# Moving 34 reversing weight copies out of the head of a tuned backward kernel, with later tables, four side jobs per call and a second-group scaling

## The chip, the cores and the metric

One core of one Trainium2 chip. Times are device microseconds (us) of the whole program. Engines: PE is TensorE, DVE VectorE, ACT ScalarE, POOL GpSimd, SP SyncE; SP issues most of the DMAs and does nothing else here.

## The reference, cut to what matters

```python
def _fwd_reference(A_x, A_w_r, A_w_i, B_x, B_w_gate, B_w_up, B_w_down, gate_w):
    x = A_x                                   # [1, 2048, 576] bf16
    g = _sigmoid((x * gate_w).sum(-1, keepdims=True))
    a = irfft2(rfft2(x) * (A_w_r + 1j * A_w_i))        # A_w: [2048, 289]
    b = (_gelu(x @ B_w_gate) * (x @ B_w_up)) @ B_w_down # [576, 4608]
    return g * a + (1 - g) * b
# reference(): this output, and the gradients of all inputs but B_x for a given grad_out (dO)
```

The kernel computes the two-dimensional transforms as matrix products with tables of angles, and the gated network (FFN) with its gradients.

## The kernel before

**The head** (0 to 87 us) loads x and dO, then the first weight block of the FFN, transforms x along one axis and then the other ("angles" Y, then "V" tiles), and stores the V tiles to DRAM. All the tiles of the transform share a pool of 19 buffers. At the end of its code stands `wrev`: 34 DRAM-to-DRAM copies that put the second half of the columns of A_w into reversed row order. POOL gets to them early and issues them from 8 to 70 us.

```python
    def reversed_rows(eng, src, dst):
        s_, d_ = (a.rearrange("(m i) (h l) -> h i m l", i=T, h=2) for a in (src, dst))
        return [lambda i=i: eng.dma_start(d_[:, i], s_[:, T - i, ::-1]) for i in range(1, T)] + \
            [...]                              # two more for i = 0
    ...
    for t in range(T):                         # head
        x1[t]()                                # angles
        ...
        if t % 3 == 0 and t + 3 < T:
            build_R(nc, tb, unit, t + 3)       # a block of tables
        if t > 0:
            x2[t - 1]()                        # V products
    build_B(nc, tb, unit, res)
    run_late(tb)
    tail_table()
    for k, v in enumerate((A_w_r, A_w_i)):
        for move in reversed_rows(nc.gpsimd, v[:, HF:DF], wrev[k][:]):
            move()
```

One such copy has the shape 2 x 128 x 72: 256 rows of 144 bytes.

**The groups** (87 to about 1030 us): 18 groups of 256 FFN columns with four iterations each. I number these 72 iterations from 0, so the second group starts with iteration 4 and the third with iteration 8. An iteration computes `z` (from `wdT`, the transposed down weights) and `xy` on PE, the activation and its derivative on ACT and DVE, weight-gradient products of the group before, and some units of the transform. In its first three iterations a group also loads the next group's weights on SP: transposes in the second (L241, L242), and in the third the copies that put the result in place, which must wait for the transposes (L245, L248). `side` holds DVE work of the transform's middle part, in small jobs; `moves` holds copies like `wrev` for the reversed halves of two outputs.

```python
    def load_w(g, part):
        if part == 0: ...                                                # wgu: six loads
        elif part == 1:
            LD.dma_start_transpose(wts[g][1][:, 4:5, :], B_w_down[fsl, DCH[4][0]:D])   # L241
            LD.dma_start_transpose(wtmp[0][:], B_w_down[fsl, 0:512])                   # L242
        else:
            LD.dma_start(wdT[LO, 4, :], wdT[HI, 4, :])                                 # L245
            ... LD.dma_start(wdT[r, 2 * par:2 * par + 2, :], wtmp[0][...])             # L248, four
    ...
            def side_work():                   # called after each half's elementwise work
                for _ in range(3):
                    if side:
                        side.pop(0)()
    ...
            if m < 3 and g + 1 < NG:
                load_w(g + 1, m)
            if (g, m) in ((0, 3), (1, 0)):
                scale_dB(T // 2)
            for _ in range(3):
                if moves:
                    moves.pop(0)()
```

**The last part** (from about 1030 us) is the last group's rest and PE products of the second phase; nothing of the change touches it.

## Time and profile before

| | before |
|---|---|
| time, median of three runs | 1491.16 us (1490.65 to 1492.24) |
| PE busy | 95% of the profiled 1494.7 us |
| start of the first z product (iteration 0) | 87.10 us |
| start of the second group (iteration 4) | 128.84 us |
| start of the third group (iteration 8) | 186.94 us |

The starts are those of the first z product (L341 on PE) of each iteration, read off the trace. Below I call "lead" how much earlier an iteration starts than in the profiled run of the kernel before. The prediction shows the profile itself.

### The profile page before, as it was taken

To read this page: it belongs to the slowest core of one execution; us is meant where nothing else is said; L and a number is where in the kernel's file an instruction comes from. 1 tells how busy PE (TensorE), PEld (TensorE's weight loads), DVE (VectorE), ACT (ScalarE), POOL (GpSimd) and SP (SyncE) were. 2 spreads that over 40 slices of the span, in tenths; PEclk is the share of its full clock that TensorE was granted. 3 is DMA by queue.
4 is the path that set the end of the run, shared out by engine and by line. 5 is a ranking of instruction groups with operands and counts; after the bars stand their busy time and mean duration, and the time that the engine had idled before them with its cause. 6 is when DMAs were issued, how large, how long until landed. Compare 5 with 4: busy or idle time off the path is not lost.

```text
span 1494.7 us, 30032 instructions
## 1 busy us (share of the span) xinstructions
PE 1414.5 (95%) x11500; PEld 1050.8 (70%) x11586; DVE 887.8 (59%) x2356; ACT 697.2 (47%) x1380; POOL 172.1 (12%) x258
## 2 busy tenths in 40 slices
PE   4388999999999999998999999999999999999997
PEld 3255767767776776776677777777877777777775
DVE  6269777988898889867677777775000461212200
ACT  3267766666667767666667667664000000000000
POOL 6500011111111111111010010010000110000000
PEclk8699999999999999999999999999999999999998
DMA  9925454455565555446556546665999998878773
GB/s 167 75 76 132 118 147 128 122 136 129 137 155 128 132 141 135 114 103 144 139 133 160 143 127 154 161 143 138 274 199 194 209 213 159 167 158 170 153 150 67
DMA packets 550712, 217.87 MB, mean 146 GB/s; under 512 B 375368, under 2 KB 540424, under 8 KB 550568
## 3 DMA queue, kind: packets, MB, share of 16 engines
q1 hardware_dynamic: 537800, 194.03, 59.4%
q0 software_dynamic: 10960, 20.91, 6.0%
q8 instruction: 90, 1.47, 0.5%
q10 hardware_dynamic: 1808, 1.02, 0.2%
q14 instruction: 54, 0.44, 0.1%
HBM read 43.28 MB, written 96.22 MB: 93 GB/s over the span
## 4 chain that ended last, share of the span: by engine, by line
PE 77%; DVE 2%; issue 1%; DMA 0%; SPq 0%; ACT 0%; DVEq 0%
PE acc L1043 28%; PE wps L464 14%; PE xy L353 12%; PE wps L447 8%; PE z L341 7%; PE wps L477 2%; PE xy L348 2%; PE z L344 1%; PE pf L745 1%; PE pf L772 1%; PE pf L774 1%; DMA pin<-scr 0%; PE pf L695 0%; PE pf L696 0%; PE pf L698 0%
## 5 line engine op out<-in xcount | busy, mean ns | idle before, releaser
L1043 PEld LDWEIGHTS <-pin 128*128 128x128 bf16 x3456 | 338.0, 98 | 86.5 <-DMA pin<-scr 1.4
L353 PE MATMUL xy<-wgu,xT 128*128 128x512 bf16 x1066 | 257.9, 380 | 10.1 <-issue 8.3
L464 PEld LDWEIGHTS <-xn 128*128 128x128 bf16 x2304 | 225.1, 98 | 31.3 <-issue 0.2
L353 PEld LDWEIGHTS <-xT 128*128 128x128 bf16 x1152 | 106.9, 98 | 139.0 <-issue 31.8
L366 ACT ACTIVATE da<-z,omg 128x256 bf16<-128x256 f32 x288 | 113.3, 474 | 126.6 <-PE z L344 123.2
L1060 ACT COPY bo<-acc 128x288 f32<-128x288 f32 x32 | 12.8, 399 | 309.3 <-PE acc L1043 284.7
L447 PE MATMUL wps<-dB,A 128*128 128x288 bf16 x1152 | 152.7, 286 | 0.0
L341 PE MATMUL z<-wdT,dOT 128*128 128x256 bf16 x1152 | 141.1, 277 | 7.0 <-DMA wdT<-wtmp 4.4
L1043 PE MATMUL acc<-wd_all,pin 128*128 128x288 bf16 x1152 | 142.8, 286 | 1.1 <-DMA pin<-scr 1.1
L1043 PE MATMUL acc<-wgT,pin 128*128 128x288 bf16 x1152 | 143.6, 286 | 0.0
L1043 PE MATMUL acc<-wuT,pin 128*128 128x288 bf16 x1152 | 143.6, 286 | 0.0
L447 PEld LDWEIGHTS <-A 128*128 128x128 bf16 x1152 | 112.6, 98 | 34.9
L464 PE MATMUL wps<-dHg,xn 128*128 128x256 bf16 x1152 | 133.1, 273 | 0.0
L464 PE MATMUL wps<-dHu,xn 128*128 128x256 bf16 x1152 | 132.0, 273 | 0.0
L341 PEld LDWEIGHTS <-dOT 128*128 128x128 bf16 x1152 | 112.5, 99 | 26.2 <-issue 6.5
L1120 DVE SCALAR_TENSOR_TENSOR f32t<-gwf,dlog,b16t 128x576 f32<-128x576 f32 x16 | 13.1, 817 | 179.2 <-DMA b16t<-dxa_scr 179.2
L372 ACT ACTIVATE q<-xy 128x512 bf16<-128x512 f32 x144 | 86.1, 598 | 66.0 <-PE xy L353 62.3
L396 ACT ACTIVATE om<-s 128x512 bf16<-128x512 bf16 x144 | 92.0, 639 | 23.7 <-DVE s L380 23.6
L470 POOL DMA_DIRECT2D out_dram<-dw x67 | 48.9, 730 | 440.7 <-ACT dw L425 290.6
L397 ACT ACTIVATE s<-s 128x512 bf16<-128x512 bf16 x144 | 90.7, 630 | 4.6
L378 ACT CAST hu<-xy 128x512 bf16<-128x512 f32 x144 | 87.0, 604 | 0.0
L379 DVE TENSOR_SCALAR s<-q 128x512 bf16<-128x512 bf16 x144 | 41.9, 291 | 73.2 <-ACT q L372 72.5
(213 smaller groups left out, 1846.8 us busy)
## 6 DMA issues: line engine op xcount, KB each, us to landing
scr<-A SPq DMA_DIRECT2D x144, 128.0 KB
scr<-dHg SPq DMA_DIRECT2D x144, 128.0 KB
scr<-dHu SPq DMA_DIRECT2D x144, 128.0 KB
out_dram<-dw POOLq DMA_DIRECT2D x67, 128.0 KB, 2.9
wd_all<-in_B_w_down_dram SPq DMA_DIRECT2D x3, 1728.0 KB
out_dram<-dwd POOLq DMA_DIRECT2D x34, 144.0 KB, 3.2
wgu<-in_B_w_gate_dram SPq DMA_DIRECT2D x18, 256.0 KB
wgu<-in_B_w_up_dram SPq DMA_DIRECT2D x18, 256.0 KB
```

The source lines that it names most:

```text
L341: nc.tensor.matmul(zo(t), lhsT=dOT[:, ci, t, :], rhs=wdT[:, ci, :], start=(t % 4 < 2 and ci == 0), stop=False)
L353: nc.tensor.matmul(xy[k][:, t % 2, :], lhsT=xT[:, ci, t, :], rhs=wgu[:, ci, :], start=False, stop=(ci == 3))
L366: nc.scalar.activation(da[:, tt, :], z[:, tt, k, :], ACT.Copy, scale=omg32[:, t:t + 1])
L372: nc.scalar.activation(q[:], xy[:, :, 0:FG], ACT.Square)
L378: nc.scalar.copy(hu[:], xy[:, :, FG:2 * FG])
L379: V.tensor_scalar(s[:], q[:], A_GELU, 1.0, op0=ALU.mult, op1=ALU.add)
L396: nc.scalar.activation(om[:], s[:], ACT.Sigmoid, scale=-2.0 * C_GELU)
L397: nc.scalar.activation(s[:], s[:], ACT.Sigmoid, scale=2.0 * C_GELU)
L447: nc.tensor.matmul(wps[:, :288], lhsT=tl(0, t)[:, fch * P:(fch + 1) * P], rhs=dB[:, t, h * 288:(h + 1) * 288], start=(t == 0), stop=(t == ...
L464: nc.tensor.matmul(wps[:, cc, :], lhsT=xn[:, t, (c0 + cc) * P:(c0 + cc + 1) * P], rhs=tl(k, t), start=(t == 0), stop=(t == T - 1))
L470: wst[0].dma_start(ov[:, c0:c0 + TPB, fsl], dw[:])
L1043: nc.tensor.matmul(acc[:, :288], lhsT=src[:, r, :], rhs=w_of(r)[:, h * 288:(h + 1) * 288], start=(first and r == 0), stop=(last and r == F ...
```

## The change

It takes `wrev` out of the head and puts it on SP, five copies per iteration until all are out, in the seventh iteration; builds tables and V products one step later; moves the tail table into an empty slot of the transform; puts every second early V copy on ACT; scales dO in the second group, with the products that use it after it; spreads the output copies; and does four side jobs per call.

```diff
         if g == 0:
-            return [[w[0], tl_], [w[1], d[0]], [d[1], d[2], d[3]], [w[2], w[3]], []]
+            return [[w[0], tl_], [w[1], w[2]], d, [w[3]], []]
...
-                if src is xT or t < 8:
+                if src is xT or (t < 8 and t % 2):
                     V.tensor_copy(Vt[:], vps[:, :, :2 * HF])
...
-                    if p == T // 2 - 1:
-                        for k, v in enumerate((out_2, out_3)):
-                            moves.extend(reversed_rows(LD, orev[k][:], v[:, HF:DF]))
+                        moves.extend(reversed_rows(orev[k][:], (out_2, out_3)[k][:, HF:DF], [(T - i) % T for i in (i0, i0 + 1)]))
...
-        if t % 3 == 0 and t + 3 < T:
-            build_R(nc, tb, unit, t + 3)
+        if t % 3 == 1 and t + 2 < T:
+            build_R(nc, tb, unit, t + 2)
...
-        if t > 0:
-            x2[t - 1]()
+        if t > 1:
+            x2[t - 2]()
+    x2[T - 2]()
...
-    tail_table()
-    for k, v in enumerate((A_w_r, A_w_i)):
-        for move in reversed_rows(nc.gpsimd, v[:, HF:DF], wrev[k][:]):
-            move()
+    for i in range(T):
+        for k, v in enumerate((A_w_r, A_w_i)):
+            moves.extend(reversed_rows(v[:, HF:DF], wrev[k][:], [i]))
...
-                for _ in range(3):
+                for _ in range(4):
                     if side:
                         side.pop(0)()
...
-            if (g, m) in ((0, 3), (1, 0)):
+            if (g, m) in ((1, 0), (1, 1)):
                 scale_dB(T // 2)
-            for _ in range(3):
+            for _ in range(5 if pr < 8 else 2):
                 if moves:
                     moves.pop(0)()
```

`pr` is the number of the iteration.

More of the change, by code (lines that the diff above doesn't have):

```diff
@@ L548, in tail_table @@
         nc.gpsimd.memset(tb.At2[:], 0.0)
-        pool, tag = headps()
-        tp_ = pool.tile([P, 2, 1024], BF16, tag=tag, name="tp")
+        tp_ = pz.tile([P, 2, 1024], BF16, tag="z", name="tp")
         for c in range(2):
@@ L582, in tiles_of, with reversed_rows @@
         return t[:].rearrange("(m i) l -> m i l", i=T)
-    def reversed_rows(eng, src, dst):
+    def reversed_rows(src, dst, tiles):
         s_, d_ = (a.rearrange("(m i) (h l) -> h i m l", i=T, h=2) for a in (src, dst))
-        return [lambda i=i: eng.dma_start(d_[:, i], s_[:, T - i, ::-1]) for i in range(1, T)] + \
-            [lambda: eng.dma_start(d_[:, 0, 1:P], s_[:, 0, P - 1:0:-1]), lambda: eng.dma_start(dst[0:1], src[0:1])]
+        out = []
+        for i in tiles:
+            if i:
+                out.append(lambda i=i: LD.dma_start(d_[:, i], s_[:, T - i, ::-1]))
+            else:
+                out.append(lambda: LD.dma_start(d_[:, 0, 1:P], s_[:, 0, P - 1:0:-1]))
+                out.append(lambda: LD.dma_start(dst[0:1], src[0:1]))
+        return out
     a_dv = a_scr[:].rearrange("(m i) d -> m i d", i=T)
@@ L829 @@
     mid = mid_units()
-    fft = fg + [gap] * 5 + mid[:-2] + pa + mid[-2:] + [gap] * 2 + ia[:-4] + pb + ia[-4:] + ib
+    fft = fg + [tail_table] + [gap] * 4 + mid[:-2] + pa + mid[-2:] + [gap] * 2 + ia[:-4] + pb + ia[-4:] + ib
     fft_pos = [0]
@@ L954 @@
                 LD.dma_start(gwb[:], gate_w.partition_broadcast(P))
-            if (g, m) in ((0, 3), (1, 0)):
+            if (g, m) in ((1, 0), (1, 1)):
                 scale_dB(T // 2)
-            for _ in range(3):
+            for _ in range(5 if pr < 8 else 2):
                 if moves:
                     moves.pop(0)()
+            assert pr != 8 or not moves
             if done[0] == n_slots or (pr >= wgT_from and pr % 2 == 0 and len(wgT_all) < 20):
```

## The prediction

> **What bounds the kernel now.** I read the page first: engine shares, then the 40 slices. TensorE ("PE") is busy 95% of 1494.7 us, and from the third slice on its row stands at 9. So a microsecond can be won only where PE is idle, and that is nearly all at the start.
>
> ```profile
> PE   4388999999999999998999999999999999999997
> PEclk8699999999999999999999999999999999999998
> DMA  9925454455565555446556546665999998878773
> ```
>
> A slice is 37 us: PE is 40% and 30% busy in the first two, while DMA is at 90% in both. I then asked for busy time by stage: the load, the hole, the rest of the head, the first group of the FFN, the second.
>
> ```profile
> 0.00:20.00 20.00, 10.24 (x78) 7.30 (x79) 13.98 (x39) 9.48 (x18) 16.45 (x33) 0.83 0.89 257
> 20.00:58.00 38.00, 8.23 (x78) 6.20 (x77) 9.05 (x20) 5.86 (x10) 19.65 (x19) 0.66 1.14 64
> 58.00:87.00 29.00, 23.62 (x286) 18.23 (x286) 16.96 (x43) 16.49 (x27) 7.01 (x8) 0.85 0.63 74
> 87.00:129.00 42.00, 37.30 (x240) 22.17 (x244) 32.35 (x90) 32.56 (x63) 0.00 (x0) 0.96 0.39 108
> 129.00:187.00 58.00, 55.74 (x445) 39.86 (x448) 46.48 (x133) 39.99 (x78) 4.46 (x7) 1.00 0.44 121
> ```
>
> Columns: stretch, length, busy us of PE, weight loads, DVE, ACT, POOL, then clock, DMA share, GB/s. From 20 to 58 us PE works 8.23 of 38 us, and DMA is fully busy while it moves only 64 GB/s. The waits of that stretch say why PE stands, and the DMA queue's order of issue says why the store it waits for is late.
>
> ```profile
> PE fx L530 <- ACT Y L519: 30.6, 2, 29.2
> ACT Rt L152 <- DMA scr_x<-Vt: 28.1, 1, 28.1
> ...
> 19.97 3.62 SPq L241 DMA_TRANSPOSE wdT<-in_B_w_down_dram  x1
> 23.64 4.16 SPq L242 DMA_TRANSPOSE wtmp<-in_B_w_down_dram  x1
> 34.24 0.50 SPq L245 DMA_DIRECT2D wdT<-wdT  x1
> 39.25 6.83 SPq L248 DMA_DIRECT2D wdT<-wtmp  x4
> 46.18 34.00 SPq L541 DMA_DIRECT2D scr_x<-Vt  x14
> ...
> q1 hardware_dynamic: 3333, 1.53, 67.8%
> q0 software_dynamic: 1842, 0.86, 45.3%
> ```
>
> The FFT's tiles share 19 "unit" buffers; about 29 us in, they are all taken by V tiles waiting to be stored. The stores stand behind the first weight block on the in-order SP queue: the issue of L245 waits for a transpose to land, L248 for the next, and the first scr_x store goes out at 46.18 and frees a buffer at 55.5. Meanwhile the 34 reversing copies of A_w (wrev, issued by POOL from 8 to 70 us) hold 45.3% of the DMA engines' time. The same block for the second group, without wrev, runs: transposes issued at 113.17 and 114.40, L245 at 123.47, L248 in 2.64 us. So the hole is DMA contention passed on through buffers.
>
> **What the Trainium skill says.** (1) "DMA: Bandwidth & Descriptors", section "Issuing engines are not separate DMA queues": DMAs of all issuers end on the same 16 engines and interleave. The trace agrees: both queues together are booked at 113% from 20 to 58 us. (2) The same page, "Why a DMA increments its semaphore by 16 and not by 1": an SP-issued DMA is split over the largest k up to 16 that divides the slowest non-unit dimension of both patterns. A reversing copy is 2x128x72, so k = 2: its 256 rows of 144 B go to two engines. The kernel already issues such copies from SP, for its outputs; the trace agrees by rate: in 641 to 642 us, when little else runs, the hardware queue is at 7.2%, near one of 16 engines. (3) "Queues, rings and completion order", same page: one ring per engine for all of SP's DMAs, taken in order. So each later 16-engine DMA of SP has a sixteenth behind a copy on those two rings. (4) "TensorE: Matmul & The Clock Gate", "What's actually happening": an idle PE falls to half clock. The trace agrees: the clock was 0.50 from 40 to 60 us.
>
> **The change, part by part.**
>
> *wrev leaves the head.* L241 is issued when the loads of dO have landed, about 17.5 us with no second queue. By the second group's pace the transposes land some 5 us later (23.5), L245 and L248 take 3.5 us (27), and the first scr_x store lands near 30. In the new program the first instruction to wait for it comes an iteration earlier than before (the angles of the fourth table block), at about 25. So 29 us of hole becomes some 5 us, with work resuming at 30 in place of 58.
>
> *The rest of the head.* 58.8 to 87.1 is 28.3 us now. V products one iteration later and table blocks one later mean PE waits less for ACT's Y copies; the tail table (eight small transposes, 1.2 us of PE, four DVE copies, 0.9 us) moves to an empty slot of the FFN, and the clock stays up. Against that, one more iteration of about 1.8 us is left after the stall. I take 27 us: the first group starts at 57 in place of 87.1. Gain 30.
>
> *DVE in the first group.* Four of 0.75 us V copies go to ACT, and the eight scalings of dO (2.32 us) to the second group: 5 us off DVE where it is busy 32 of 42 us, worth perhaps 2 us by itself. The reordered dO products are the same PE work.
>
> *wrev enters SP in the first two groups, five per iteration.* The build has them right after that iteration's weight block. The cost of three such copies can be read where the outputs are reversed, late in the kernel:
>
> ```profile
> 695.24 1.28 SPq L242 DMA_TRANSPOSE wtmp<-in_B_w_down_dram  x1
> 696.57 3.93 SPq L587 DMA_DIRECT2D out_dram<-orev  x3
> 700.61 2.09 SPq L412 DMA_DIRECT2D scr<-A  x1
> ...
> 706.42 0.55 SPq L245 DMA_DIRECT2D wdT<-wdT  x1
> 707.02 2.63 SPq L248 DMA_DIRECT2D wdT<-wtmp  x4
> ...
> 709.90 0.58 PE L341 MATMUL z<-wdT,dOT 128*128 128x256 bf16 x2 [3.81 <-DMA wdT<-wtmp]
> ```
>
> The DMA packet records give 768 packets of 144 B in 7.0 us for three, so 2.34 us for one on its two rings. From the end of L242 to L245 it is 9.9 us, the last copy's landing included, and PE then waited 3.81 us for the weights. Five copies need 11.7 us of those rings per iteration; the other traffic of an iteration takes about 5.5 there (share 0.39 to 0.44 of 10 to 14.5 us). That is 17 us in iterations of 10 to 14.5: SP falls behind.
>
> Second group's weights, from the first group's start: L242 ends at about 32 (29.6 now), plus 9.9 and two further copies of 2.34 gives L245 at 46.6; L248 lands 4.6 later at 51. The group now starts at 41.8, so 9 us are lost, the DVE gain with them. Third group: by the time its L248 lands, the two rings have served 28 full copies (65 us), seven iterations of stores (25), two weight blocks (13), and were idle for the first 20: 123 us. It starts now at 186.9 - 87.1 = 99.8. So the loss has grown to 23 or 24. After the seventh iteration no copies are left.
>
> *Output copies spread.* They go out four per row pair during the middle of the transform, not 34 in a row from 635 to 790 us, where the weight waits cost PE 4.4 us and one iteration took 18.3 us in place of about 14. I count 5 us back. Four side jobs per call, not three, have no PE wait to remove.
>
> Sum: 30 - 24 + 5 + 1 (rounding of the small moves) = 12 us, so 1491 - 12 = 1479.
>
> **The rivals.** *A: the copies are hidden as SP's other traffic is.* For it: buffers are deep (16 dHg/dHu, 13 A), and three per iteration over twelve iterations cost only 4.4 us of PE waits. Then 30 + 5 + 3 are kept and the time is about 1455. Against it: 11.7 + 5.5 exceeds an iteration, 7 + 5.5 does not. *B: the hole stays,* because the transposes or the 512 B weight rows are slow by themselves next to the 4.7 MB of loads. For it: the page's GB/s fall only after the loads. Against it: the second group's block at normal pace. With a resumption at 45 the head would gain 15, and the total would be near 1494. *C: DVE bounds the first group,* so the scaling and V copies are the gain: at most 5 us, as PE idles 4.7 of the 42 us there.
>
> **Range and chances.** The head's gain is 30 give or take 5, the loss at the group starts 24 give or take 8, the late part 5 give or take 3; together about 10 either way, a little less where an earlier start only meets the same wait for the weights: 1463 to 1490. Over 2% faster needs 1461, which takes rival A for more than half: 12%. Slower by 2% needs the hole to stay and the copies to cost: 1%.
>
> **What would show it.** Right: no wrev on POOL; PE's hole at 25 to 58 down to a few us; first z product near 57; then SP's L245 of the second group over 14 us after its L242, PE waits of about 9 and 14 us on wdT at the two next group starts, and no such wait after 200 us. Wrong: no weight wait there (rival A, time under 1461); or a scr_x store still landing after 40 us (rival B). If the first z product is at 57 but groups two and three take 42 and 58 us as now, the ring arithmetic is what failed.

## The result, and the profile after

| | before | after |
|---|---|---|
| time, median of four runs | 1490.91 us (1489.52 to 1492.24) | 1493.98 us (1491.51 to 1494.16) |
| ratio after/before | | 1.0017, 95% interval 1.0000 to 1.0034 |
| PE busy | 95% | 95% |
| first z product | 87.10 us | 48.97 us |

A ratio here is the mean time of one kernel's fast runs over that of the other's of the same rounds, so it isn't quite the ratio of the medians. The time did not move, 15 us above the prediction and above its range. But the profile moved a good deal. The slices of the profile's second part, of the kernel after:

```profile
PE   7859599899999999999999999999999999999997
PEclk9989799999999999999999999999999999999999
DMA  6234464345555564465445546565999998877773
```

The hole of the first two slices is gone, and DMA is no longer full there. In its place two new dips stand in PE's row, the third and fifth slices (75 to 112 and 149 to 187 us), with DMA at 3 to 4 tenths only: PE waits, and no bandwidth is short.

First the head. The SP queue's order of issue there, and the longest wait for a store in all engines' waits from 15 to 49 us:

```profile
21.09 0.49 SPq L245 DMA_DIRECT2D wdT<-wdT  x1
21.68 2.65 SPq L248 DMA_DIRECT2D wdT<-wtmp  x4
24.43 23.51 SPq L541 DMA_DIRECT2D scr_x<-Vt  x15
```

```profile
DVE CR L146 <- DMA scr_x<-Vt: 3.0, 1, 3.0
```

L245 goes out at 21.09 us in place of 34.24, the first V tile's store at 24.43 in place of 46.18, and the wait of 28.1 us for a free buffer is 3.0. The first z product starts 38.1 us earlier.

Then the loss. PE's waits from 80 to 185 us (who waits for whom: us in total, times, longest), then the SP queue in the window of the second group's weight block:

```profile
PE z L341 <- DMA wdT<-wtmp: 28.9, 4, 14.7
```

```profile
82.76 1.28 SPq L242 DMA_TRANSPOSE wtmp<-in_B_w_down_dram  x1
84.09 0.67 SPq L589 DMA_DIRECT2D wrev<-in_A_w_i_dram  x1
...
88.08 2.84 SPq L589 DMA_DIRECT2D wrev<-in_A_w_r_dram  x1
90.96 2.65 SPq L589 DMA_DIRECT2D wrev<-in_A_w_i_dram  x1
93.72 2.56 SPq L541 DMA_DIRECT2D scr_g<-Vt  x1
...
100.55 0.54 SPq L245 DMA_DIRECT2D wdT<-wdT  x1
101.14 2.65 SPq L248 DMA_DIRECT2D wdT<-wtmp  x4
```

Columns: start, us, queue, line, what is moved. The first two copies take under 1 us of the queue; from the third on each takes 2.3 to 2.8, and so does the store after them: about what the prediction had estimated for one copy on its two rings, 2.34. From 86 to 96 us the hardware queue that SP feeds (q1) moves 1125 packets, all of them under 512 bytes, at 16 GB/s and 15.2% of the time of 16 engines, that is of 2.4 engines: what else SP has issued hardly moves. Between the end of L242 and L245 lie 16.5 us (before: some 7 us, from 116.6 to 123.47), and PE, with nothing else to do, waits 12.91 us at 104.04. There is no such wait in the kernel before at these two group starts. The stretch after it costs something too:

```profile
178.24 0.59 PE L341 MATMUL z<-wdT,dOT 128*128 128x256 bf16 x2 [14.73 <-DMA wdT<-wtmp]
179.45 3.15 PE L341 MATMUL z<-wdT,dOT 128*128 128x256 bf16 x14 [0.62 <-DMA wdT<-wtmp]
```

These 14 products take 3.15 us; at the full clock 16 of them take 1.9. From 170 to 178 us the granted clock was 0.50. This is what the Trainium skill says in "TensorE: Matmul & The Clock Gate", section "What's actually happening": an idle PE falls to half clock, and gets the full one back after some microseconds of work. So a wait at a group start costs more than its length.

The lead over the kernel before, from the profiled run of each kernel that follows (us; columns are iterations):

| kernel | 0 | 3 | 4 | 8 | 16 | 18 | 47 | 49 |
|---|---|---|---|---|---|---|---|---|
| after | 38.1 | 36.6 | 24.8 | 8.7 | 4.5 | 2.4 | -7.5 | -0.7 |
| e1_side3 | 38.4 | 36.8 | 26.0 | 9.9 | 5.4 | 5.4 | 5.0 | 11.8 |
| e2_pool | 38.0 | 36.4 | 25.5 | 24.3 | 23.1 | 20.0 | 10.5 | 17.3 |
| e3_pool_side3 | 39.7 | 38.1 | 27.6 | 26.7 | 25.7 | 25.7 | 25.8 | 32.6 |
| e4_vdve | 38.5 | 39.7 | 27.3 | 11.2 | 6.4 | 4.3 | -5.2 | 1.6 |
| e6_poolhead | 9.4 | 7.8 | 6.9 | 8.2 | 6.8 | 4.2 | -5.7 | 1.1 |
| e9_before_one | 36.9 | 36.9 | 36.9 | 36.9 | 36.9 | 34.2 | 32.7 | 30.4 |
| e7_one | 38.3 | 36.7 | 35.8 | 37.0 | 35.8 | 33.2 | 8.9 | 15.7 |
| e8_one_s3_v | 39.8 | 40.9 | 41.0 | 41.7 | 40.6 | 38.2 | 13.9 | 20.7 |
| e12_straight | 39.7 | 38.2 | 34.4 | 33.3 | 32.0 | 29.2 | 19.8 | 26.6 |
| e5_three | 39.8 | 38.2 | 37.3 | 37.8 | 26.5 | 23.8 | 14.4 | 21.2 |
| e11_before_side4 | 5.5 | 5.7 | 5.7 | 5.7 | 5.1 | 4.2 | -5.6 | -6.9 |
| e10_skip_s3_v | 38.4 | 39.5 | 39.6 | 40.2 | 31.8 | 30.3 | 12.4 | 19.2 |
| e13_pool_m03_s3_v | 37.8 | 38.3 | 38.3 | 39.0 | 36.5 | 36.6 | 36.1 | 42.9 |

Read the first row: 38.1 won in the head; 33.6 lost by iteration 16, all of it by iteration 10; 12.0 lost from iteration 16 to 47, in small steps; 6.8 won back in iterations 47 and 48; nothing after that. The sum is -0.7. One caution: e11's head is that of the kernel before, and still starts 5.5 us earlier, so the kernel with the hole varies by some microseconds from run to run. The last part varies too: it took 472.7 to 477.6 us in these profiles, though no edit touches it. So the last number of a row agrees with the difference of the median times only to within 5 us (after: 0.7 us behind by its lead, 3.1 by the medians). The steps inside a row are the better measure.

The small steps are the surprise. PE's waits from 185 to 640 us, before, then after:

```profile
PE pf L695 <- ACT da L366: 2.8, 1, 2.8
```

```profile
PE pf L698 <- ACT da L366: 7.1, 5, 1.5
PE z L341 <- ACT Vt L703: 5.9, 3, 4.4
```

And DVE in one and the same iteration around 405 us, before, then after:

```profile
407.06 0.76 DVE L644 TENSOR_TENSOR n<-Xg,Wt 128x1156 bf16<-128x1156 bf16 x1
407.73 0.29 DVE L379 TENSOR_SCALAR s<-q 128x512 bf16<-128x512 bf16 x1
```

```profile
405.78 1.43 DVE L649 TENSOR_TENSOR n<-Xg,Wt 128x1156 bf16<-128x1156 bf16 x2
...
408.18 0.84 DVE L665 TENSOR_TENSOR qn<-n 128x576 bf16<-128x576 bf16 x2
408.93 0.18 DVE L666 COPY qn<-n 128x8 bf16<-128x8 bf16 x1
409.00 0.29 DVE L379 TENSOR_SCALAR s<-q 128x512 bf16<-128x512 bf16 x1
```

L379 is the first of the elementwise work of the iteration, on whose result ACT waits, and on ACT's `da` in turn PE. In both traces DVE runs this work in the order of the program. With three jobs a call, one multiplication is ahead of it; with four, the rest of the job is there too, down to the folding into qn, and L379 starts at 409.00 although z of that iteration started 0.36 us earlier than before. DVE was not short of time, but its order was changed.

### The profile page after: what moved, and what is told of

The parts are those of the page before. It is cut to its first block, busy times and chain, and to the rows that moved or that the text cites. A ratio compares the mean times of both kernels' runs of the same rounds, so it can differ in the third digit from the quotient of the medians.

```text
span 1492.3 us, 30020 instructions
## 1 busy us (share of the span) xinstructions
PE 1414.1 (95%) x11500; PEld 1049.8 (70%) x11586; DVE 884.5 (59%) x2352; ACT 698.2 (47%) x1384; POOL 136.1 (9%) x224
## 4 chain that ended last, share of the span: by engine, by line
PE 57%; issue 0%; DVE 0%; ACT 0%; DVEq 0%
PE acc L1047 28%; PE wps L464 8%; PE xy L353 7%; PE wps L447 5%; PE z L341 4%; PE wps L477 1%; PE pf L748 1%; PE xy L348 1%; PE z L344 1%; PE pf L775 1%; PE pf L777 1%; PE pf L761 0%; ACT da L366 0%; DVE n L649 0%; PE pf L698 0%
## 5 line engine op out<-in xcount | busy, mean ns | idle before, releaser
L341 PE MATMUL z<-wdT,dOT 128*128 128x256 bf16 x1152 | 142.4, 278 | 39.2 <-DMA wdT<-wtmp 28.9
L379 DVE TENSOR_SCALAR s<-q 128x512 bf16<-128x512 bf16 x144 | 42.3, 294 | 78.5 <-ACT q L372 77.8
```

What stands on the lines that cost most here:

```text
L341: nc.tensor.matmul(zo(t), lhsT=dOT[:, ci, t, :], rhs=wdT[:, ci, :], start=(t % 4 < 2 and ci == 0), stop=False)
L379: V.tensor_scalar(s[:], q[:], A_GELU, 1.0, op0=ALU.mult, op1=ALU.add)
```

## The experiments

Thirteen kernels ran, all with outputs that passed the comparison with the reference. The theories at the start: **R**, the 33.6 us go to the two rings that five copies per iteration fill; **S**, the 12 us go to the fourth side job; **D**, the second group's weights are late for another reason, the copies only coincide. Later ones are named where they come up. Each "before" is of the same rounds.

### e1: three side jobs

```diff
-                for _ in range(4):
+                for _ in range(3):
                     if side:
```

> The changed kernel with three side jobs per call, as before, not four. Theory S (four product jobs in a row on DVE hold up the FFN's chain, so ACT reads z late and PE waits once per row pair): between iterations 16 and 47 the changed kernel lost 12.0 us on the one before; they come back, and the time is about 1482. Rival M (that loss comes from the output copies that are now spread over the same stretch): the time stays at 1494.

1481.61 us (before 1494.1), ratio 0.993, interval 0.990 to 0.996. The lead stays at 4.9 to 5.4 from iteration 16 to 47 (but for iteration 17, at 2.8), where that of the kernel after falls by 12. S holds, to half a microsecond.

### e2: the copies on POOL, paced

```diff
+            if pr < 8 and moves:
+                nc.gpsimd.tensor_copy(pace[:], kept[g][-1][2][:, 0, 0:1])   # waits for this iteration's dHu
             for _ in range(5 if pr < 8 else 2):
                 ...                          # wrev: nc.gpsimd.dma_start in place of SP's
```

> The changed kernel with the reversing copies of A_w issued by POOL, not SP, five per iteration in the same iterations (a one-column copy on POOL that waits for the iteration's last dHu paces them). Theory R (what hurt is that on SP's own in-order rings the weights of the next group stood behind these copies): the first z product stays near 49 us, the waits of z for wdT at the second and third group (28.9 us) all but vanish, iterations 4 to 9 are no slower than before; about 33 us back, so about 1461. Rival D (the copies load the DMA engines whoever issues them, as they did in the head of the kernel before): more than half of the wait stays, 1480 or more.

1475.75 us (before 1494.1), ratio 0.988, interval 0.984 to 0.992. Neither: the loss at the third group is gone, that at the second stays (lead 36.4 to 25.5). The SP queue says that the weights were late there again, by another way:

```profile
79.29 1.38 SPq L242 DMA_TRANSPOSE wtmp<-in_B_w_down_dram  x1
...
92.76 1.83 SPq L245 DMA_DIRECT2D wdT<-wdT  x1
94.64 6.46 SPq L248 DMA_DIRECT2D wdT<-wtmp  x4
```

and the stretches say what was different (84 to 104 us: length, busy us of PE, weight loads, DVE, ACT, POOL, then clock, DMA share, GB/s; after, then e2):

```profile
84.00:104.00 20.00, 6.69 (x42) 3.33 (x40) 13.98 (x38) 9.62 (x18) 0.00 (x0) 0.78 0.38 87
```

```profile
84.00:104.00 20.00, 7.43 (x45) 3.56 (x43) 14.89 (x39) 9.73 (x19) 9.25 (x11) 0.77 0.96 97
```

With the copies on SP the 16 engines are 38% busy and PE starves all the same; with them on POOL the engines are 96% busy at nearly the same GB/s, and the four L248 take 6.46 us in place of 2.65. That leaves open whether POOL's copies do it (call it **C**, contention) or D. e13 decides.

### e3: both

e1 and e2 together.

> Both edits together. If R and S hold and are separate stretches of time, the gains add: 1494 - 33 - 12 = about 1449, near 3% faster than the kernel before. If one of the two gives nothing, 1461 or 1482.

1463.08 us, ratio 0.980, interval 0.977 to 0.984. 12.7 us below e2: the gains add. The miss of 14 us is e2's.

### e4: early V copies on DVE again

```diff
-                if src is xT or (t < 8 and t % 2):
+                if src is xT or t < 8:
```

> The changed kernel with all of the early V copies on DVE, as before. The first group's iterations were 10.9 us, against 10.1 before. Theory A (the copies made ACT the bound there): the iterations go back to 10.1 to 10.3, but the second group still waits for wdT, so the time stays within 1.5 us of 1494. Rival (the longer iterations come from something else, as DMA or the z buffer): they stay at 10.9, same time.

1492.7 us, ratio 1.0003, interval 0.997 to 1.003. The first four iterations are back to the pace of the kernel before, and a little over it (the lead rises from 38.5 to 39.7, where after's falls from 38.1 to 36.6). Of the 3.1 us that this is ahead of after at iteration 3, 2.5 are left at iteration 4 and 1.9 at iteration 16: the wait at the second group (13.9 us in place of 13.6) and small steps after it take the rest. A difference of 1.3 us in the medians is too small to say more.

### e6: the copies back in the head

The kernel after, with `wrev` issued by POOL in the head, at once.

> The changed kernel with one part undone: the 34 reversing copies of A_w are issued by GpSimd in the head again, all at once; table order, V copies, dO scaling, side work and output moves stay as changed. Theory H (the head's 38 us come from the copies leaving it): the first z product is back near 85 us, no wait for wdT at the second and third group, and the time is about 1491 + 12 (side work) - 7 (late part) = 1496 us. Rival O (the earlier tables and later angles carry a good part of the head's gain): first z product between 60 and 75 us, time between 1470 and 1486 us.

1493.68 us (before 1496.03), ratio 0.998, interval 0.995 to 1.002. The hole is back (the first scr_x store goes out at 45.98 us), the two waits are gone. The first z product starts at 77.7, not at 85: later tables and angles are worth 9.4 us in this profile, of which up to 5.5 can be the head's variation.

### e9: before, with the copies alone moved, slowly

The kernel before, with `wrev` on SP at a pace that fits its use: in the kernel before, the first pair of rows is read at 215.7 us and the last at 546.2.

```diff
-    for k, v in enumerate((A_w_r, A_w_i)):
-        for move in reversed_rows(nc.gpsimd, v[:, HF:DF], wrev[k][:]):
-            move()
+    wmoves = [...]                            # the same copies, in order of use
...
+            for _ in range(0 if pr < 4 else 2 if pr < 7 else 1):
+                if wmoves:
+                    wmoves.pop(0)()
```

> The kernel before with one thing changed: the 34 copies leave the head and go out on SyncE from the second group on, two per iteration for three iterations and then one, since the first pair of them is read near 190 us and the last near 540 us. Theory H: first z product at 50 to 55 us, no wait for wdT of over 2 us at a group start, time 1491 - 34 = about 1457 us. Rival O: first z product at 60 to 75 us and a time of 1466 to 1480 us.

1465.21 us (before 1496.03; expected 1457), ratio 0.979, interval 0.976 to 0.983. The first z product starts at 50.18 us: of the 38 us, 36.9 come from the copies leaving the head, with the old order of tables. So e6's 9.4 and these 36.9 overlap; a better order helps a head with a hole, and hardly one without. The lead is kept to the last decimal up to iteration 17. 4.3 us are lost from iteration 17 to 19 (PE there waits on ACT's `da` and `Vt`, not on weights), and 2.3 at 47 to 49, where the 34 output copies in a row are still in the program.

### e7 and e8: the slow pace in the kernel after

e7 is the kernel after with e9's pace for `wrev`. e8 also has three side jobs and all early V copies on DVE.

> The changed kernel with the same slow pace for the copies on SyncE (none before the second group, then two per iteration for three iterations, then one) and nothing else. Theory R (five copies per iteration are more than their two rings and the queue carry, and that is the whole loss at the two group starts): no wait for wdT of over 2 us at the second and third group; 33 us come back, time about 1461 us. Rival D (the second group's weight block is late for another reason, since with the copies on GpSimd PE still waited 12 us there): a wait of some 10 us stays at the second group start, time 1470 us or more.

> The changed kernel with the slow pace of the copies, three side jobs per call as before, and all early V copies on VectorE as before: everything that the runs blamed is taken out, the rest stays. If the parts add: 1461 - 12 (side work) - 1.5 (V copies, now not taken back by a wait for weights) = about 1447 us, ratio to the kernel before 0.971. If the V copies only shift a wait, 1449 us.

e7: 1481.19 us, ratio 0.989, interval 0.985 to 0.994. e8: 1470.67 us, ratio 0.983, interval 0.979 to 0.987. At the second and third group R is right and D wrong: no wait for wdT, the lead is 37.0 and 41.7 at iteration 8. But both miss the expected time, by 20 and 24 us: between iterations 24 and 36 PE waits for wdT again, 9.7 us in e7 and 16.7 in e8, and e8's lead falls from 38.0 at iteration 23 to 13.8 at iteration 38. The SP queue of e8 at the block of iteration 24, between L242 and L245:

```profile
352.62 0.69 SPq L589 DMA_DIRECT2D wrev<-in_A_w_r_dram  x1
353.42 3.89 SPq L589 DMA_DIRECT2D out_dram<-orev  x2
```

From about 300 us on the spread output copies go out two per iteration; with one `wrev` copy that makes three in the weight block's window. Two alone cost no wait for wdT in the kernel after, e1, e2 and e3; three cost up to 8.9 us in one wait. I had stretched one stream of copies into the time of the other.

### e12: as many copies, forward rows

The kernel after with the rows not reversed, so that the outermost dimension is the 128 and not the 2 (a wrong result; A_w is so small here, about 0.001, that the comparison with the reference doesn't notice).

```diff
-            moves.extend(reversed_rows(v[:, HF:DF], wrev[k][:], [i]))
+            s_, d_ = (a.rearrange("(m i) l -> i m l", i=T) for a in (v[:, HF:DF], wrev[k][:]))
+            moves.append(lambda i=i, s_=s_, d_=d_: LD.dma_start(d_[i], s_[(T - i) % T]))
...                                          # as before, a copy of row 0 alone follows for i = 0
```

> The changed kernel with the copies of A_w not reversed (a wrong result on purpose): as many copies at the same five per iteration on SyncE and as many bytes, but each of 128 rows that run forward, so that its outermost dimension is 128 and not 2[...]. Theory R (it is the two rings that are full): no wait for wdT of over 2 us at the second and third group, the 33 us come back there, first group to fourth at the pace of the kernel before, time about 1461 us. Rival Q (it is the number of DMAs in the one queue of SyncE[...], whatever they move): the waits of about 13 and 14 us stay, time 1485 us or more.

1467.17 us (before 1491.86), ratio 0.984, interval 0.982 to 0.986. The same queue at the same place as shown of the kernel after:

```profile
86.07 0.60 SPq L826 DMA_DIRECT2D wrev<-in_A_w_i_dram  x1
86.76 0.54 SPq L541 DMA_DIRECT2D scr_g<-Vt  x1
```

A copy now takes 0.60 us of the queue in place of up to 2.84, and the store after it 0.54 in place of 2.56. Of the lead, 7.7 us are lost by iteration 16 in place of 33.6: 26 us come back, so the copies' shape carries most of the loss, and Q is false as the main cause. But a wait of 5.0 us stays at the second group. Most of it is e12's own doing: its copies for i = 0 write row 0, which the next copy writes again, so SP waits for them to land, 1.6 and 3.0 us (`prof e12_straight --waits --engine SP --window 66:82`; nothing of the kind in the kernel after). Five copies are also 3.2 us of queue time by themselves, but whether any wait comes of the number of DMAs isn't shown. The Trainium skill asks for this shape ("DMA: Bandwidth & Descriptors", "Rules for kernel authors": a dimension that is a multiple of 16, ideally the 128, outermost), and the trace agrees: from 85 to 88 us the hardware queue takes 40.5% of the time of 16 engines, in the kernel after 15.2% beside the same copies. Bytes and number of DMAs are the same as in the kernel after, but the rows are joined to 288 bytes, so the number of rows is half; the test doesn't separate that from the spread over the engines.

### e5: three copies per iteration

```diff
-            for _ in range(5 if pr < 8 else 2):
+            for _ in range(3 if pr < 12 else 2):
```

> The changed kernel with three copies per iteration in the first twelve iterations, not five in the first seven. Theory R: three take 7.0 us of the two rings and the rest of the traffic some 5.5, 12.5 in all, against iterations of 11 to 14; waits for wdT of 3 to 5 us at the second, third and fourth group, together about 12 us where five copies lost 33; time about 1473 us. If the loss goes by the total of the copies and not by their rate, it stays at 1485 us or more.

1474.22 us (before 1491.86), ratio 0.989, interval 0.986 to 0.991. The time is right, its parts are not: at the second and third group there is next to no wait, and one of 6.8 us at the fourth (lead 36.7 at iteration 11, 26.7 at iteration 13), where the loads of the transform's middle part begin as well. The loss goes by the rate, not by the total of the copies: by iteration 16 five per iteration lost 33.6 us, three 13.3, and two and then one (e9) nothing. Where and how much three cost depends on what else is in the queue.

### e11: before with four side jobs

> The kernel before with four side jobs per call in place of three, and nothing else. Theory S (the fourth job puts one more VectorE job ahead of the elementwise work that PE waits for, about 1.5 us per row pair and some 5 us at the first): 10 to 12 us slower, about 1503 us. If the loss in the changed kernel came only from its own order of the weight products or of the loads, no change: 1491 us.

1502.78 us (before 1491.86), ratio 1.0079, interval 1.006 to 1.010. 11 us slower, with this one digit changed. S needs nothing else of the change.

### e10: three per iteration, none beside the transposes

The kernel after with three side jobs, V copies on DVE, and `for _ in range(0 if pr < 4 or m == 1 else 3)` on SP.

> A candidate for the best: the changed kernel with three side jobs, early V copies on VectorE, and the copies of A_w on SyncE from the second group on, three per iteration but none in the iteration between the transposes and the loads of a weight block, so that they are all out before the output copies begin near 300 us. Theory R: no wait for wdT at any group start; the first z product at 47 us, 40 us ahead of the kernel before, kept through, and 6.8 us more near 700 us: 1491 - 47 = about 1445 us, ratio 0.968. If three copies still reach the next weight block, or collide with the loads of the first row pairs near 190 us, 1455 us or more.

1472.61 us, ratio 0.987, interval 0.985 to 0.990: a miss of 28 us. The first two group starts are clean, but the copies last until iteration 19, and from there they meet the loads of the first row pairs. One wait of 4.2 us at iteration 14:

```profile
PE pf L618 <- DMA Vp<-scr_x: 4.2, 1, 4.2
```

then 3.9 and 6.3 us on wdT from 260 to 345 and from 345 to 400 us. At the second of these no `wrev` copy is left, but SP's queue is late: the transposes of that weight block go out 32.5 us after the start of their iteration, number 21, where e13 below, with as many output copies and side jobs, issues them after 20.1. That a queue which once fell behind by an iteration had not caught up is the likely cause; no run tests it.

### e13: the copies on POOL, outside the weight block's window

```diff
+            if pr < 12 and m in (0, 3) and moves:
+                nc.gpsimd.tensor_copy(pace[:], kept[g][-1][2][:, 0, 0:1])
+            for _ in range((6 if m in (0, 3) else 0) if pr < 12 else 2):
```

and three side jobs, V copies on DVE. This was also the candidate for the best.

> The changed kernel with three side jobs, early V copies on VectorE, and the copies of A_w issued by GpSimd six at a time, only in the last iteration of a group and the first of the next (held back by a one-column copy of that iteration's dHu), so that none is in flight while a weight block moves, and all are out by the twelfth iteration. If the 12 us wait for wdT that stayed at the second group with the copies on GpSimd came from their packets beside the weight block (theory C), it is under 2 us here; the first z product is at 48 us, its 39 us lead is kept through the first four groups but for about 1 us, 6.8 us more near 700 us: 1491 - 46 = about 1445 us, ratio 0.969. If that wait came from something else in the early start (rival D), it stays near 11 us and the time is about 1456 us.

1451.63 us (1449.95 to 1453.56; before 1492.9), ratio 0.972, interval 0.970 to 0.974. No wait for wdT at the second group, and the same stretch as above now reads:

```profile
84.00:104.00 20.00, 18.01 (x140) 11.77 (x139) 18.93 (x51) 16.25 (x31) 5.77 (x7) 1.00 0.67 154
```

PE is busy 18.01 of 20 us in place of 7.43. So C is right: the 12 us that stayed in e2 were POOL's copies beside the weight block. (The V copies, which differ from e3 too, don't remove such a wait: e4 has 13.9 us of it.) It beats both kernels by some 41 us and is the only run whose interval lies below 0.98. Of the 6.6 us to the expected 1445, 1.9 are lead (36.1 at iteration 47, where 38 was expected) and 1.9 the slower kernel before of these rounds; the rest lies in the sum of the expectation and in the last part.

## Why the prediction was wrong, step by step

- *The hole is DMA contention passed on through buffers, and leaves with wrev.* Right (e9 alone: 36.9 us), and under-sized: I took 57 us for the first z product, it was 48.97. Work was to resume at 30 and hardly stopped in fact (a wait of 3.0 us). Term: 30 give or take 5, measured 38.1 (with e11's head in place of before's it would be 32.6).
- *Second group: 9 us lost; third: grown to 23 or 24.* The mechanism was right: SP's order, two rings, and waits for wdT at just these two starts (12.9 and 14.7 us; I had said about 9 and 14). Under-sized: 33.6 in place of 24 give or take 8. The two waits with their small second parts are 28.9, V copies on ACT 1.5, and the rest is some 3 us. That fits PE's half clock after each wait, which the sum did not have: without their waits, the 16 z products after each took 3.8 and 3.7 us, not 1.9. L245 came 51.6 us after the first group's start where I had 46.6. One reading behind it was weak: 7.2% from 641 to 642 us is no sign of k = 2, which would be two engines of 16, 12.5%; the same kind of copies from 699 to 703 us are at 18.8%.
- *DVE in the first group: perhaps 2 us.* Wrong in sign: with the V copies on ACT the lead falls by 1.5 us in the first three iterations, where with them on DVE it rises by 1.1 (e4, e8, e10); PE's waits for ACT's Y copies at iterations 1 and 2 came to 2.9 us. By iteration 16 the V copies are a loss of 1.5 us (33.6 lost in after, 32.1 in e4).
- *Output copies spread: 5 us back.* Right; 6.8 measured. e9 and e11, which don't spread them, win nothing there (they lose another 2.3 and 1.3 us).
- ***Four side jobs per call, not three, have no PE wait to remove.*** This is the step that failed. The sentence is true and the conclusion, a cost of nothing, is not: there was no wait to remove, but one to make. It cost 12.0 us in the profile, 12.4 between after and e1, 11 alone (e11). I had looked for waits that the fourth job would take away, and not at what stood behind the side jobs in DVE's order.
- *Sum.* 30 - 24 + 5 + 1 was 12. Measured, from the profile: 38.1 - 33.6 - 12.0 + 6.8 = -0.7. That the first two terms net to about what I had (6 predicted, 4.5 measured) is luck: by the profile each lies outside the range that I gave it. What is left of the miss is the side jobs. With three of them the time is 1481.6, against the predicted 1479, by the same luck. The 1 us for rounding has no counterpart. The range was loosely drawn too: "about 10 either way" of 1479 is not 1463 to 1490.
- *Rivals.* A (copies hidden) is false at five per iteration and true for two; B (the hole stays) and C of the prediction (DVE bounds the first group) are false.
- *What would show it.* The listed signs for "right" came, but for the size of two: no wrev on POOL, the hole gone, L245 16.5 us after L242, waits on wdT at two starts (12.9 and 14.7 us, not 9 and 14) and none after 200 us; the first z product was at 49 us, not near 57. None of the signs looked at the middle of the kernel, which is why they could come beside a wrong time.

## What to carry to other kernels

A DMA stream that is moved out of one crowded place needs a place and a pace: look up when its result is first read (here 129 us after the head, and then bit by bit for 330 us), and keep it out of the window in which PE's next weights travel. An in-order engine with time to spare can still make the bound engine wait, so check what stands behind each piece of work that is added to it. When several gains and losses ride on one change, compare the start of every iteration between the two traces: it gives each part its own number, even when the total says that nothing happened.

## What the Trainium skill lacked or had wrong

- "DMA: Bandwidth & Descriptors", "Why a DMA increments its semaphore by 16 and not by 1": it gives the rule for k, but not what a small k does to those behind it in the queue. Here copies of k = 2 by that rule made the issue of a following ordinary store take 2.56 us in place of 0.54 (after against e12, whose rows are also twice as long), with the 16 engines 38% busy.
- The same page, "Issuing engines are not separate DMA queues": it says that issuing on several engines saves only the sequencer's time, which is usually small. Here it was not small: one copy took up to 2.84 us of SP's queue, and the same 34 copies, moved from SP to POOL at the same pace, took 18 us off the time (1475.75 against 1493.98), and with the weight block's window kept free another 11 (e3 to e13, of which the V copies can be some 2). That both end on the same engines holds: they also cost 12 us where they met a weight block.
- The same page has no figure for what many short rows issued from POOL do beside another queue's work: the stretch with some ten such copies went from a DMA share of 0.38 to 0.96 (after against e2), while the bytes moved hardly rose (87 to 97 GB/s).
